# The last tail of a transformer block: projections planned among the value products, transposes two to a bank, fewer idle products, a fourth bank for the up products

## The chip, the cores and the metric

The kernel runs on one core of one Trainium2 chip. The metric is the device time of one launch in microseconds, median of three runs. Beside it one execution was recorded by the hardware profiler; all times within the kernel are taken from that one, counted from the start of its span.

## The reference

One transformer block on 2048 tokens of width 512, in bf16. A vector c gives six modulation rows; the first half is attention with 32 heads of 16, the second a dense layer pair with a GELU between:

```
mod = silu(c) @ w_mod            -> sa, ca, ga, sb, cb, gb
h = layernorm(x) * (1 + ca) + sa
x = x + ga * (softmax(q k^T / 4) v) @ wo      with q, k, v from h @ wqkv
h = layernorm(x) * (1 + cb) + sb
out = x + gb * (gelu(h @ w1 + b1) @ w2 + b2)  with 1376 inner columns
```

## The kernel before

**The stream.** The tokens are four blocks of 512. For each block the 32 heads are treated in eight groups of four, so there are 32 groups ("quads", `nq` = 32). A group needs scores against 16 tiles of keys. Twelve of these tiles go through ScalarE's exponential in units of three and two banks (tiles sA and sB in PSUM, pA and pB out of them, lines 1063 and 1115); the others through an approximation on VectorE (lines 1181 and 1210, tile t), whose scores go into one of two single banks called aux. The value products (`do_pv`, line 1267) add everything up in one bank called od. When a group is done, its od is divided by its denominators and becomes a tile OT.

**The planner.** Python code plays through the whole attention with assumed durations and writes the instructions in the order in which it would start them. At each step `pe_step` chooses what TensorE gets: scores, value products, a step of a "job", or, if nothing is due, `do_fill` (line 1290): four products of zeros into od, which only keep TensorE busy. Jobs are everything else: projections of q, k and v, and for each finished block its tail (output projection, layer norm, both dense layers). A job has a due time `at`, counted in groups, a list of steps, and labels that it needs; a job that holds an aux bank keeps any other such job from starting. The chip then runs each engine's queue in the written order, with waits on semaphores between engines.

**The last block.** Its tail can't hide behind later attention. Two jobs `last_oproj(0)` and `last_oproj(1)` (due at 31.0 and 31.05) make the output projections of token tiles 0 and 1 in the two aux banks: an identity product that brings in the residual xr, then one product for each OT tile t = 0 to 6 (`o_mm`, lines 741 and 742). The product of t = 7 waits for the last group. `do_out` treats this group apart: the denominators are spread by a shuffle (line 1315), inverted (`recip`, 1318) and multiplied in (`norm`, 1321), first for tokens 0 to 255; the rest is handed to `last_tail` in pieces: `last["recip"]`, `last["norm"]`, and `last["out"]`, which copies od to o_sbL (line 1299) and sends the denominators over two transfers on SP's queue (d, then dall) for a test of their range at the end.

`last_tail` writes the rest by hand. Its order for TensorE before: t = 0 to 6 of token tile 2 in a bank of `fpo`; `keep_on(KEEP[0])`, four idle products into a bank that nobody reads (line 795); t = 7 of tiles 0 and 1; tile 3; six more idle products (`KEEP[1]`). Then the block is treated in two halves of 256 tokens. `norm_half` takes the statistics on VectorE (line 799), copies x1 (the tile xr) on ScalarE (800), and normalizes to hnL (274). `begin_down` (lines 842 and 843) puts the residual and the bias into the output banks. `transposes` turns hnL by chunks of 128 columns (line 279, two products to a chunk) and evacuates them with scale and shift to h2T (316 on ScalarE, 319 on VectorE). `up_half` makes eleven products of 256 tokens (line 817, four instructions each) and a GELU on ScalarE for each (819, tile uG). `down_tile` (line 824, eleven instructions) ends a token tile; it is copied (828 or 830) and stored through SP (831).

The banks of transposes and up products come in turn from the list `own`: three of the pool `fps` (name fb) and od's as the fourth, which is in the turn only once `span[0]` is 4:

```
own = [(fps, "fb"), (fps, "fb"), (fps, "fb"), (psO, "od")]
turn, span = [], [3]
```

The first idle product's bank and each transposed chunk take a place in the turn. The order of the second part is this:

```
norm_half(0); begin_down(0), begin_down(1)
last["recip"](256, 384); transposes(0)
last["recip"](384, 512); last["norm"](256, 512)
up_half(0, range(5)); t = 7 of tiles 2 and 3; norm_half(1)
up_half(0, range(5, 11)); begin_down(2), begin_down(3)
down_tile(0); transposes(1); down_tile(1)
last["out"](); span[0] = 4
up_half(1, range(11)); range_flag(); down_tile(2); flag; down_tile(3)
```

Of the kernel before, what the change touches and what calls it, by code (L numbers as in the profile page):

```python
# [25 lines left out]
NC = 4  # L26
# [33 lines left out]

WARM = 18

KEEP = (4, 6)

POOL_WAIT = 3.0

# [32 lines left out]
def adaln_block(ctx: ExitStack, tc: tile.TileContext, A_x, A_wqkv, A_wo, B_x, B_w1, B_b1, B_w2, B_b2,  # L99
# [644 lines left out]

    def last_oproj(tt):

        def f(part):
            def g(j):
                if part == 0:
                    j.ps = last[tt] = j.alloc()  # L750
                for t in range(2 * part, min(7, 2 * part + 2)):
                    o_mm(j.ps, tt, t)
            return g
        job(8 * NQB - 1.0 + 0.05 * tt, [(PE_, n * MM, f(i)) for i, n in enumerate((3, 2, 2, 1))],
            ["last", "d_done"] + [("ot", NQB - 1, t) for t in range(7)], ("last", tt), 99)

    for tt in range(2):
        last_oproj(tt)
# [2 lines left out]
    def last_tail():  # L761

        b = NQB - 1
        tl, tl2 = late["tl"], late["tl2"]
        W_1, W_2, b1c = late["W_1"], late["W_2"], late["b1c"]
        x1 = last["xr"]
        h2 = tl.tile([P, NC, 512], BF16, name="h2T")
        uG = tl.tile([P, NFC, 512], BF16, name="uG")
        hnp = ctx.enter_context(tc.tile_pool(name="hnp", bufs=2))
        hn2 = [hnp.tile([P, 4, D], BF16, name="hnL") for _ in range(2)]  # L770
        st = tl.tile([P, 4, 6], FP32, name="st2")
        with tc.tile_pool(name="fpo", bufs=2, space=PSUM) as fpo, \
                tc.tile_pool(name="fps", bufs=3, space=PSUM) as fps:

            own = [(fps, "fb"), (fps, "fb"), (fps, "fb"), (psO, "od")]
            turn, span = [], [3]

            def bank(dt=FP32, n=512):
                if not turn:
                    turn.extend(range(span[0]))  # L780
                pool, nm = own[turn.pop(0)]
                return pool.tile([P, n], dt, name=nm)

            early = tl.tile([P, 1], FP32, name="early")
            nc.scalar.activation(out=early, in_=eps_c, func=ACT.Sqrt)
            po = [last[0], last[1]] + [fpo.tile([P, 512], FP32, name="fo") for _ in range(2)]
            for t in range(7):
                o_mm(po[2], 2, t)


            idle = bank()

            def keep_on(n):
                for _ in range(n):
                    nc.tensor.matmul(out=idle, lhsT=ident, rhs=hT[:, 0, 0:512], start=True, stop=True)
            def norm_half(hf):
                tts = (2 * hf, 2 * hf + 1)
                for tt in tts:
                    nc.vector.bn_stats(out=st[:, tt, :], in_=po[tt])
                    nc.scalar.copy(out=x1[:, tt, :], in_=po[tt])  # L800
                mv, rs = (ln_rstd if hf else ln_sqrt)(st[:, 2 * hf:2 * hf + 2, :], 2)
                for i in range(2):
                    ln_norm(x1, hn2[hf], mv, rs, 2 * hf + i, i)

            def transposes(hf):
                for j in range(NC):
                    pst = bank(BF16, 256)
                    transpose_chunk(pst, hn2[hf], j, (2 * hf, 2 * hf + 1))
                    hT_evac(h2[:, j, 256 * hf:256 * hf + 256], pst, 8 + j,
                            "act" if j % 2 and not hf else "dve")  # L810

            def up_half(hf, fcs):
                cs = slice(256 * hf, 256 * hf + 256)
                for fc in fcs:
                    ps = bank(FP32, 256)
                    for j in range(NC):
                        nc.tensor.matmul(out=ps, lhsT=W_1[:, j, fc * P:(fc + 1) * P], rhs=h2[:, j, cs],
                                         start=(j == 0), stop=(j == NC - 1))
                    nc.scalar.activation(out=uG[:, fc, cs], in_=ps, func=ACT.Gelu_apprx_tanh,
                                         bias=b1c[:, fc:fc + 1], scale=1.0)  # L820

            def down_tile(tt, eng=None):
                for fc in range(NFC):
                    nc.tensor.matmul(out=po[tt], lhsT=uG[:, fc, tt * P:(tt + 1) * P], rhs=W_2[:, fc, :],
                                     start=False, stop=(fc == NFC - 1))
                o = tl2.tile([P, D], BF16, name="ob")
                if eng == "act":
                    nc.scalar.copy(out=o, in_=po[tt])
                else:
                    nc.vector.tensor_copy(out=o, in_=po[tt])  # L830
                nc.sync.dma_start(out=out_tok[4 * b + tt], in_=o)

            keep_on(KEEP[0])
            for tt in (0, 1):
                o_mm(po[tt], tt, 7)
            for t in range(7):
                o_mm(po[3], 3, t)
            keep_on(KEEP[1])

            def begin_down(tt):  # L840

                nc.tensor.matmul(out=po[tt], lhsT=ident, rhs=x1[:, tt, :], start=True, stop=False)
                nc.tensor.matmul(out=po[tt], lhsT=ones_row, rhs=late["b2r"], start=False, stop=False)
            norm_half(0)

            nc.scalar.activation(out=early, in_=b1c[:, 0:1], func=ACT.Gelu_apprx_tanh)
            for tt in (0, 1):
                begin_down(tt)
            last["recip"](256, 384)
            transposes(0)  # L850
            last["recip"](384, 512)
            last["norm"](256, 512)
            up_half(0, range(5))
            for tt in (2, 3):
                o_mm(po[tt], tt, 7)
            norm_half(1)
            up_half(0, range(5, NFC))
            for tt in (2, 3):
                begin_down(tt)
            down_tile(0)  # L860
            transposes(1)
            down_tile(1)
            last["out"]()
            span[0] = 4
            up_half(1, range(NFC))
            bad, onec, fl = range_flag()
            down_tile(2)
            pf = bank(FP32, 1)
            nc.tensor.matmul(out=pf[0:1, :], lhsT=bad, rhs=onec, start=True, stop=True)
            nc.vector.tensor_copy(out=fl, in_=pf[0:1, :])  # L870
            down_tile(3, "act")
# [254 lines left out]
    def progress():  # L1126

        return act_prog[0]
# [287 lines left out]
    def pe_step():  # L1416
        m = mode[0]
        ready = qk_ready()
        its = next_unit()
        if its is None or not all(quad_labels(qi, kt) for qi, kt, _ in its):  # L1420
            slack = INF
        else:

            slack = max(act_pending() - 0.45, exp_end.get(unit["u"] - 2, act_pending()) + SEM) - clock
        if ready and (m == "row" or slack < 0.35):
            rows = do_qk()
            if d_ready():
                r = d_row(rows)
                if r is not None:
                    do_d(r, True)  # L1430
            return True
        dr = d_ready()
        if dr and m == "row" and (free[DVE_] <= clock + 0.5):
            do_d(d_row(()), False)
            return True
        todo = pv_list()
        n = len(todo)
        if ready and not (m == "col" and n and slack > 0.5):
            rows = do_qk()
            if dr:  # L1440
                r = d_row(rows)
                if r is not None:
                    do_d(r, True)
            return True
        o = job_for(PE_)
        late_ = o is not None and o.at + 0.3 < progress()
        if o is not None and (late_ or n < 3) and (o.rows[o.i][1] + SWITCH <= slack + 0.25 or late_):
            do_job(o, PE_)
            return True
        if n and (m == "col" or n >= 3 or todo[0][0] + 1.5 < clock):  # L1450
            do_pv(todo[0][1], todo[0][2])
            return True
        if dr and free[DVE_] <= clock + 0.4:
            do_d(d_row(()), False)
            return True
        if o is not None and o.rows[o.i][1] + SWITCH <= slack + 0.3:
            do_job(o, PE_)
            return True
        if n:
            do_pv(todo[0][1], todo[0][2])  # L1460
            return True

        while pe_log and pe_log[0][0] < clock - FILL_SPAN:
            pe_log.popleft()
        return slack > FILL_SLACK and sum(d for _, d in pe_log) < FILL_SHARE * FILL_SPAN and do_fill()
# [106 lines left out]
```

## Time and profile before

| | |
|---|---|
| median of 3 runs | 811.74 us (811.29 to 812.61) |
| the profiled execution | 814.66 us |
| its span | 812.8 us |
| mean granted TensorE clock | 0.991 |
| TensorE products (PE), weight loads (PEld) | 769.4 us busy (95%), 235.2 us (29%) |
| VectorE (DVE), ScalarE (ACT) | 714.6 us (88%), 755.1 us (93%) |
| GpSimd (POOL) | 84.4 us (10%) |

Busy times by stretch of the last part, in microseconds:

| stretch | PE | DVE | ACT | clock |
|---|---|---|---|---|
| 760.0 to 770.0, attention | 9.98 | 9.85 | 10.00 | 1.00 |
| 770.0 to 775.3, first projections | 5.25 | 0.39 | 3.56 | 1.00 |
| 775.3 to 784.0, last group, first half's norm | 8.35 | 6.66 | 3.14 | 1.00 |
| 784.0 to 792.0, up products of the first half | 6.85 | 5.33 | 6.64 | 1.00 |
| 792.0 to 803.0, down, up of the second half | 10.18 | 3.26 | 4.05 | 1.00 |
| 803.0 to 812.8, last down tiles, store | 5.18 | 2.71 | 1.38 | 0.91 |

A share over the span says little about this kernel's last part: the stretches have different limits. In a line of the timeline stand start, length, engine, line, operation, tile written and tiles read; "x12" joins instructions that follow one another; brackets give the engine's idle time before it and the engine and line that ended it. Products are pipelined: a product of 512 columns shows 0.38 us, while the next one starts earlier than that.

### The profile page before, as it was taken

How to read it: one execution, taken by the hardware profiler on the slowest of the kernel's cores; microseconds unless marked ns; L12 is line 12 of the kernel's file. 1: busy time of each engine (PE TensorE's matmuls, PEld its weight loads, DVE VectorE, ACT ScalarE, POOL GpSimd, SP SyncE). 2: the span in 40 equal slices, each digit the busy share in tenths (PEclk: the TensorE clock that was granted, in tenths of full speed). 3: DMA queues.
4: the chain of work that ended last, by engine and by line, in shares of the span. 5: the costliest groups of instructions: out<-in, count | busy, mean ns of one | idle time of the engine just before them, and what ended most of it. 6: DMA issues, size and time to landing. Idle time of an engine off the chain costs nothing.

```text
span 812.8 us, 18189 instructions
## 1 busy us (share of the span) xinstructions
PE 769.4 (95%) x7383; PEld 235.2 (29%) x7453; DVE 714.6 (88%) x1260; ACT 755.1 (93%) x681; POOL 84.4 (10%) x126
## 2 busy tenths in 40 slices
PE   6999999997999999999999999999999999999997
PEld 3332222222222223222223222222222322222244
DVE  6779999999998999998999999998997989898752
ACT  4898999997998999999999999999998999999952
POOL 1100002024322000000001000000001000000000
PEclk9999999999999999999999999999999999999999
DMA  9100001022100000000100000000100000000100
GB/s 299 39 1 16 15 16 26 21 94 73 40 16 15 16 15 2 21 23 21 48 15 17 16 14 5 20 22 22 49 15 16 15 13 9 11 28 23 48 0 30
DMA packets 30283, 24.50 MB, mean 30 GB/s; under 512 B 13457, under 2 KB 24050, under 8 KB 30194
## 3 DMA queue, kind: packets, MB, share of 16 engines
q1 hardware_dynamic: 29506, 22.49, 9.6%
q8 instruction: 60, 0.98, 0.5%
q10 hardware_dynamic: 688, 0.79, 0.3%
q14 instruction: 29, 0.24, 0.1%
HBM read 20.65 MB, written 2.61 MB: 29 GB/s over the span
## 4 chain that ended last, share of the span: by engine, by line
PE 53%; ACT 26%; DVE 10%; issue 9%; DMA 2%; POOL 0%; SPq 0%; ACTq 0%; POOLq 0%; DVEq 0%
PE od L1267 16%; ACT pA L1115 13%; ACT pB L1115 10%; PE sA L1063 7%; PE sB L1063 7%; PE aux L1063 4%; DVE t L1210 4%; DVE t L1181 4%; PE aux L713 3%; PE od L1290 3%; PE aux L650 2%; PE aux L688 2%; PE aux L338 1%; ACT uG L702 1%; PE aux L324 1%
## 5 line engine op out<-in xcount | busy, mean ns | idle before, releaser
L1115 ACT ACTIVATE pA<-sA 128x1536 bf16<-128x1536 f32 x309 | 468.3, 1516 | 13.8 <-PE sA L1063 7.0
L1181 DVE TENSOR_SCALAR t<-aux 128x512 int16<-128x512 f32 x504 | 331.8, 682 | 36.6 <-PE aux L1063 35.0
L1115 ACT ACTIVATE pB<-sB 128x1024 bf16<-128x1024 f32 x309 | 336.8, 1090 | 8.2 <-PE sB L1063 4.3
L1210 DVE TENSOR_SCALAR t<-t 128x2048 int16<-128x2048 int16 x378 | 261.1, 713 | 4.0 <-PE od L1267 1.5
L1063 PE MATMUL aux<-qm,kT 32*128 32x512 bf16 x504 | 180.0, 382 | 1.8 <-DVE t L1181 0.8
L1063 PEld LDWEIGHTS <-kT 32*128 32x128 bf16 x2048 | 77.7, 91 | 271.5 <-issue 266.3
L1267 PE MATMUL od<-pB,VE 128*32 128x512 bf16 x617 | 141.4, 388 | 2.8 <-DVE o_sb L1299 2.8
L1267 PE MATMUL od<-pA,VE 128*32 128x512 bf16 x927 | 142.3, 387 | 0.6 <-DVE o_sb L1299 0.5
L1267 PE MATMUL od<-t,VV 128*32 128x512 f16 x1512 | 139.7, 386 | 2.3 <-DVE t L1210 1.9
L1063 PE MATMUL sA<-qm,kT 32*128 32x512 bf16 x927 | 122.6, 384 | 11.9 <-ACT pA L1115 7.7
L1063 PE MATMUL sB<-qm,kT 32*128 32x512 bf16 x617 | 121.4, 385 | 6.3 <-ACT pB L1115 2.6
L1399 POOL COPY mark<-t 1x1 int16<-1x1 int16 x51 | 10.4, 203 | 635.4 <-DVE t L1210 443.5
L1267 PEld LDWEIGHTS <-VE 128*32 128x32 bf16 x2048 | 48.4, 94 | 94.4 <-issue 84.2
L1290 PE MATMUL od<-hT,zeros 128*32 128x512 bf16 x836 | 75.4, 384 | 0.0
L1267 PEld LDWEIGHTS <-VV 128*32 128x32 bf16 x1512 | 40.9, 95 | 57.0 <-issue 46.6
L1267 PE MATMUL od<-t,VE 128*32 128x512 f16 x504 | 50.1, 387 | 1.2 <-DVE o_sb L1299 0.9
L1343 POOL TENSOR_TENSOR OT<-o_sb,rb 128x512 bf16<-128x512 f32 x31 | 39.4, 1271 | 5.4 <-DMA rb<-d 3.9
L713 PE MATMUL aux<-W,uG 128*128 128x512 bf16 x119 | 35.8, 383 | 1.7 <-issue 1.7
L688 PE MATMUL aux<-h2T,W 128*128 128x512 bf16 x113 | 35.4, 384 | 0.7 <-issue 0.6
L1290 PEld LDWEIGHTS <-zeros 128*32 128x32 bf16 x864 | 21.6, 95 | 35.0 <-issue 29.7
L693 DVE TENSOR_SCALAR uG<-aux,b1c 128x512 bf16<-128x512 f32 x33 | 24.6, 744 | 2.3 <-PE aux L688 2.2
L650 PE MATMUL aux<-W_o_pad,OT 128*128 128x512 bf16 x86 | 25.4, 382 | 0.7 <-issue 0.3
(164 smaller groups left out, 433.5 us busy)
## 6 DMA issues: line engine op xcount, KB each, us to landing
rb<-d SPq DMA_DIRECT2D x124, 64.0 KB
W_m<-in_w_mod_dram SPq DMA_DIRECT2D x2, 1024.0 KB
xr<-in_A_x_dram SPq DMA_DIRECT2D x4, 512.0 KB
out_dram<-ob SPq DMA_DIRECT2D x16, 128.0 KB
xb<-in_A_x_dram SPq DMA_DIRECT2D x3, 512.0 KB
W<-in_B_w_dram SPq DMA_DIRECT2D x1, 1376.0 KB
W<-in_B_w_dram SPq DMA_DIRECT2D x1, 1280.0 KB
W_m<-in_w_mod_dram SPq DMA_DIRECT2D x1, 512.0 KB
```

What stands on the lines that cost most here:

```text
L650: nc.tensor.matmul(out=j.ps, lhsT=OT[(b, t)][:, tt * P:(tt + 1) * P], rhs=W_o_pad[:, t, :], start=False, stop=(t == 7))
L688: nc.tensor.matmul(out=j.ps, lhsT=late["W_1"][:, c, fc * P:(fc + 1) * P], rhs=T["h2"][:, c, :], start=(c == 0), stop=(c == NC - 1))
L693: nc.vector.tensor_scalar(out=T["u"][:, fc, :], in0=j.ps, scalar1=late["b1c"][:, fc:fc + 1], scalar2=None, op0=ALU.add)
L713: nc.tensor.matmul(out=j.ps, lhsT=T["u"][:, fc, tt * P:(tt + 1) * P], rhs=late["W_2"][:, fc, :], start=False, stop=(fc == NFC - 1))
L1063: nc.tensor.matmul(out=dst, lhsT=kT[32 * r:32 * r + 32, ch, kt * P:(kt + 1) * P], rhs=qm[(b, ch)][32 * r:32 * r + 32, par, :], start=True, ...
L1115: nc.scalar.activation(out=pt[:, 0:n, :], in_=st[:, 0:n, :], func=ACT.Exp, scale=math.log(2.0) / STEP)
L1181: nc.vector.tensor_scalar(out=t0[(qi, kt)][:, r, :], in0=sd, scalar1=T_BIAS, scalar2=0.0, op0=ALU.add, op1=ALU.max)
L1210: nc.vector.tensor_scalar(out=t16, in0=t0[(qi, kt)], scalar1=float(MJ[j]), scalar2=None, op0=ALU.add)
L1267: nc.tensor.matmul(out=od[qi][32 * r:32 * r + 32, :], lhsT=w, rhs=src, start=first, stop=last_)
L1290: nc.tensor.matmul(out=dst[32 * r:32 * r + 32, :], lhsT=zeros, rhs=hT[:, r, 0:512], start=bank is not None, stop=bank is not None)
L1343: nc.gpsimd.tensor_tensor(out=OT[(b, t)], in0=o, in1=j.rb, op=ALU.mult)
L1399: nc.gpsimd.tensor_copy(out=mark[0:1, 0:1], in_=dve_now["prev"][0:1, 0:1])
```

## The change

- The two `last_oproj` jobs get one step per OT tile instead of two, and stop at t = 5; t = 6 is written in `last_tail`, ahead of the idle products. They need six OT tiles to start instead of seven.
- `pe_step`: when the job at hand is due after `nq - 1.1` (only these two are), value products that are ready go first, and the job is not treated as late.
- `KEEP` falls from (4, 6) to (2, 1).
- `transposes` puts chunks 0 and 2 into one bank and 1 and 3 into another; both chunks of a bank are written ahead of its two evacuations.
- `last["out"]` and `span[0] = 4` move ahead of the first half's up products, and three of these instead of five stand ahead of t = 7 of tiles 2 and 3.

```diff
-KEEP = (4, 6)
+KEEP = (2, 1)
...
-        def f(part):
+        def f(t):
             def g(j):
-                if part == 0:
+                if t == 0:
                     j.ps = last[tt] = j.alloc()
-                for t in range(2 * part, min(7, 2 * part + 2)):
-                    o_mm(j.ps, tt, t)
+                o_mm(j.ps, tt, t)
             return g
-        job(8 * NQB - 1.0 + 0.05 * tt, [(PE_, n * MM, f(i)) for i, n in enumerate((3, 2, 2, 1))],
-            ["last", "d_done"] + [("ot", NQB - 1, t) for t in range(7)], ("last", tt), 99)
+        job(8 * NQB - 1.0 + 0.05 * tt, [(PE_, (1 + (t == 0)) * MM, f(t)) for t in range(6)],
+            ["last", "d_done"] + [("ot", NQB - 1, t) for t in range(6)], ("last", tt), 99)
...
-                for j in range(NC):
-                    pst = bank(BF16, 256)
-                    transpose_chunk(pst, hn2[hf], j, (2 * hf, 2 * hf + 1))
-                    hT_evac(h2[:, j, 256 * hf:256 * hf + 256], pst, 8 + j,
-                            "act" if j % 2 and not hf else "dve")
+                for odd in range(2):
+                    pst = bank(BF16, 512)
+                    for i, j in enumerate((odd, odd + 2)):
+                        transpose_chunk(pst[:, 256 * i:256 * i + 256], hn2[hf], j, (2 * hf, 2 * hf + 1))
+                    for i, j in enumerate((odd, odd + 2)):
+                        hT_evac(h2[:, j, 256 * hf:256 * hf + 256], pst[:, 256 * i:256 * i + 256], 8 + j,
+                                "act" if odd and not hf else "dve")
...
+            for tt in (0, 1):
+                o_mm(po[tt], tt, 6)
             keep_on(KEEP[0])
...
-            up_half(0, range(5))
+            last["out"]()
+            span[0] = 4
+            up_half(0, range(3))
             for tt in (2, 3):
                 o_mm(po[tt], tt, 7)
             norm_half(1)
-            up_half(0, range(5, NFC))
+            up_half(0, range(3, NFC))
             for tt in (2, 3):
                 begin_down(tt)
             down_tile(0)
             transposes(1)
             down_tile(1)
-            last["out"]()
-            span[0] = 4
...
         late_ = o is not None and o.at + 0.3 < progress()
+        if o is not None and o.at > nq - 1.1:
+
+            if n:
+                do_pv(todo[0][1], todo[0][2])
+                return True
+            late_ = False
```

## The prediction

> **What bounds the kernel now.** I read the page first (its clock row and its shares by engine), then the timeline of the last 45 us, because every edit lies there, then the chain of waits for the same stretch, and last the windows of the start, for the clock.
>
> The page's rows say that TensorE is busy 95% of the span and the granted clock stands at 9 tenths or more in every slice. The chain of the last stretch runs almost wholly over TensorE, so here the order of its queue is the time. The timeline shows what stands in that order (start, length, engine, line, tile):
>
> ```profile
> 766.32 0.82 PE L1290 MATMUL od<-hT,zeros 128*32 128x512 bf16 x12
> 768.75 0.60 PE L1290 MATMUL od<-hT,zeros 128*32 128x512 bf16 x8
> 771.32 0.75 ACT L1115 ACTIVATE pB<-sB 128x512 bf16<-128x512 f32 x1
> 775.31 0.40 PE L1267 MATMUL od<-pA,VE 128*32 128x512 bf16 x3
> ...
> 777.38 1.03 PE L795 MATMUL fb<-hT,ident 128*128 128x512 bf16 x4
> 778.06 0.43 DVE L1321 TENSOR_TENSOR OT<-od,rbL 128x256 bf16<-128x256 f32 x1
> 778.54 0.60 PE L742 MATMUL aux<-W_o_pad,OT 128*128 128x512 bf16 x2
> 780.71 1.46 PE L795 MATMUL fb<-hT,ident 128*128 128x512 bf16 x6
> 781.32 0.73 DVE L274 TENSOR_SCALAR hnL<-xr,mv,rs 128x512 bf16<-128x512 bf16 x2
> 783.28 0.51 PE L279 MATMUL fb<-ident,hnL 128*128 128x128 bf16 x6
> ```
>
> The last exponential ends at 771.32 + 0.75 = 772.07, yet the last value products start at 775.31: two whole projection tiles stand ahead of them. OT is ready at 778.49 and its projections (t = 7) start at once. The normalized rows hnL are done at 782.05, but six idle products and the four of begin_down hold TensorE until 783.27.
>
> ```profile
> 784.99 2.02 PE L817 MATMUL fb<-h2T,W 128*128 128x256 bf16 x17 [0.17 <-ACT h2T L316]
> 787.26 1.30 DVE L799 BATCH_NORM_STATS2 st<-fo 128x6 f32<-128x512 f32 x2 [1.61 <-PE fb L817]
> 789.07 2.51 ACT L819 ACTIVATE uG<-fb,b1c 128x256 bf16<-128x256 f32 x6
> 789.61 1.47 PE L817 MATMUL fb<-h2T,W 128*128 128x256 bf16 x12 [0.85 <-ACT uG L819]
> 794.57 0.50 PE L279 MATMUL fb<-ident,hnL 128*128 128x128 bf16 x6
> 795.83 0.27 PE L279 MATMUL fb<-ident,hnL 128*128 128x128 bf16 x2 [0.77 <-DVE h2T L319]
> 798.31 1.91 PE L817 MATMUL fb<-h2T,W 128*128 128x256 bf16 x16
> 805.58 0.08 PEld L869 LDWEIGHTS <-bad 128*1 128x1 bf16 x1 [0.42 <-DVE onec L885]
> 808.26 0.59 ACT L828 CAST ob<-fo 128x512 bf16<-128x512 f32 x1 [4.47 <-PE fo L824]
> ```
>
> The brackets are idle time and its releaser: 0.85 us for a bank held by a GELU, 0.77 us for the bank of the fourth transposed chunk. That the idle products lie on the path, the chain of waits says in a line of its own:
>
> ```profile
> 780.88 1.29 PE fb L795 x6
> ```
>
> For the clock, the windows of the start and of the tail's thinnest stretch (busy time of PE, PEld, DVE, ACT, POOL; then the granted clock, third from the right):
>
> ```profile
> 12.00:13.00 1.00, 0.49 (x2) 0.21 (x2) 1.00 (x3) 1.00 (x2) 0.00 (x0) 0.63 1.10 353
> 13.00:14.00 1.00, 1.00 (x4) 0.34 (x3) 1.00 (x2) 0.35 (x1) 0.00 (x0) 0.50 1.10 350
> 15.00:16.00 1.00, 0.94 (x3) 0.24 (x2) 0.02 (x1) 0.00 (x0) 0.00 (x0) 0.66 1.17 308
> 788.00:790.00 2.00, 1.15 (x11) 0.88 (x10) 1.76 (x9) 1.99 (x5) 0.00 (x0) 1.00 0.00 0
> ```
>
> **Units.** From start to start, a full product of 512 columns takes 0.216 us (eight from 773.49 end at 775.22), one of 256 columns 0.109 us (20 from 798.31 put the next bank's at 800.50), four value products 0.22 us, a change between full, row and column products 0.10 us, and begin_down 1.27 us. I keep a ledger of the lead: how much earlier than before the same event comes.
>
> **1. Projections among the value products.** The built program has 20 filling products fewer; 12 + 8 + 4 become 4 + two gaps used by projections. The first gap: 4 fills (0.22), change (0.10), two products (0.43), change against 12 fills (0.65) and the same last change. The scores sA come some 0.08 us later; ScalarE takes them at 767.76, so this is covered by 0.2 us. The second: one product (0.22), a change, and a value group pulled ahead puts the next sA at about 769.54 instead of 769.37; its exponential at 769.99 needs it by 769.95. The scores are done 0.39 us later, 769.93, a hand-over takes 0.04, so 0.02 us is to spare: 0 to 0.3 us on ScalarE, and I take 0. The bank that the projection takes was read at 765.49 to 766.13, before it is wanted at 766.65. The last value products can then start at 772.22, 3.1 us earlier, and VectorE has OT at 775.41. But TensorE is not free: one product for t = 5, seven for the second tile, eight for po[2], two for t = 6 and two idle ones, 20 x 0.216 = 4.32 us, end at 772.22 + 0.32 + 4.32 = 776.86. So 1.4 us of the 3.1 go into waiting for TensorE, and t = 7 starts at 776.86 against 778.54: **lead 1.68**. POOL's last OT (t = 6) ends at 771.64 and is wanted at 776.
>
> **2. Idle products 6 to 1.** Behind t = 7 come po[3] (8 x 0.216) and one idle product, up to 779.24; the copies that begin_down waits for end at 778.61 and 779.20. Transposes at 779.24 + 1.27 = 780.52; hnL is ready at 782.05 - 1.68 = 780.37. **Lead 2.75** (five idle products are 1.08).
>
> **3. Two transposes per bank.** All eight now run without a wait (0.45 us of starts plus 0.27), but no evacuation starts before the four of its bank are done, where the first began at 783.60, 0.32 after the first transposes. VectorE is not ready anyway: its reciprocal (0.95 us), queued ahead, runs 780.29 to 781.24. ScalarE's two evacuations (0.57 each) start at about 781.15 and end at 782.3; so do the first up products: 782.34 against 784.99. **Lead 2.65.**
> The Trainium skill, "PSUM — Partial Sum Buffer", section "PSUM bank collisions raise a hardware error", says that two engines must not touch one bank at once even at different addresses, which speaks against packing: an evacuation may not overlap the bank's other transposes. By it alone I would add the wait for two more transposes; the row of the reciprocal shows that wait covered on VectorE.
>
> **4. Three up products, then t = 7 of the second half.** Eight 256-column products fewer ahead of it are 0.87 us. VectorE now sets the time: evacuations 781.25 to 781.98, reciprocal to 782.93, OT to 783.30, and then the moved copy o_sbL (0.68) to 783.95, queued ahead of the statistics. Statistics start at 783.95 against 787.26: **lead 3.31**. The copy costs about 0.2 us of that, as the products would let them start at 783.77. Its two transfers pass SP ahead of the output stores; SP has nothing queued from 766.6 to 795.49.
>
> **5. Fourth bank.** The product in od waits for that copy (783.95), behind it three more products, whose GELUs wait on ScalarE behind the two casts, which wait for the statistics: nothing new. The bank that comes free first after the casts is od's, as before fb's: GELU 785.76, TensorE at 786.30 (2.35 us after the statistics, as before). Then four up products remain instead of three: 0.44 us more. **Lead 2.87** at begin_down, 788.04 against 790.91. Here ScalarE's last GELU ends at 789.3, wanted at 791.5.
>
> **6. Second half.** Before, from the transposes (794.57) to the next down tile (795.94) 1.37 us passed; now about 0.50, as each pair has its bank: **lead 3.74**. The four evacuations (1.36) hide behind down_tile(1) (2.37). The flag's 0.1 us at 805.58 may go too, as its transfers, 3.5 us from copy to landing before, now land some 7 us ahead of their reader. Behind that, down tile, cast and store are unchanged.
>
> The sum: 3.75 us off the profiled execution, 814.66 (span 812.8 and 1.86 around it) to 810.9. The median of the runs lies 2.92 under the profiled one; I take the same difference off it: 811.74 - 3.75 = 808.0.
>
> **Rivals.** *VectorE's chain is longer.* Between 777.3 and 785.2 it has hardly a gap in my ledger; each late end moves steps 3 to 5 one for one. If semaphores cost 0.05 us on each of ten steps and the first wait of step 1 costs 0.3 us, 0.8 to 1.5 us go: 809.0 (lead 2.2 to 3.0). For it: every hand-over in the timeline shows 0.02 to 0.05. Against: the same steps before carry them already.
> *The lead dies at the GELUs.* If ScalarE keeps banks longer and the up products of the first half end when they did relative to the exponentials, only steps 1 and 2 less a wait remain: 1.0 to 1.6, so about 810.4, no change that shows.
> *Slower: the clock.* At the start TensorE idles 2.73 us up to 12.51, and about 2.5 us after its last product the granted clock falls to 0.50 for some 3.4 us (windows above): 1.7 us of work lost each time. With fewer idle products a gap of that length in the tail would halve the clock; the lead of 3.75 is gone after 7.5 us at half clock, and it is 0.2% slower after 10.7 us (5.35 us lost). Four such falls in the 22 us after 782 lose 6.8 us: 814.8. It decides from a gap of about 2.5 us; the longest that I find is 1.1 us (781.2 to 782.3, with three products inside), and the 0.85 us gap in 788 to 790 kept 1.00.
> The Trainium skill, "TensorE: Matmul & The Clock Gate", section "Part 1: The HAM clock gate", gives the same gate a free-running window of about 3.4 us, and its section "Part 4: PE-mode transpose" says that transposes do not count as busy. By that, the stretch from the last full product before them (780.5) to the first up product is the dangerous one, 1.8 us; the trace of before has the same stretch (783.3 to 784.99) at clock 1.00.
> *The change doesn't do it*: the built order shows the value products ahead, so only a stall could undo it; that is the second rival.
>
> **Numbers.** Forecast (lead 3.0 to 4.3) 0.63; VectorE's chain 0.20; even more lead 0.05; lead dies 0.07; clock 0.05. A measurement of this kernel can tell 0.2%, 1.6 us. Faster 0.88, same 0.07, slower 0.05. The range reaches from 4.9 us of lead (all waits gone) to 2.0: 806.8 to 809.7.
>
> **What would show it.** Right: last value products at 772.2 to 772.5, t = 7 at about 776.9 with no wait on OT, transposes at 780.5, statistics at 784, no wait of 0.77 in the second transposes, clock 1.00 to the end. Wrong: exponentials ending after 772.4, a wait of the up products beyond 0.5 us at od, or a granted clock under 1.00 before 804.

## The result, and the profile after

The median fell from 812.61 to 806.67 us (11 runs of each; ratio 0.9938, 95% interval 0.9919 to 0.9957). That median lies 0.1 us under the range's lower end, and 5.94 us is more than the 3.75 forecast. A second set, run with the experiments below, gave 810.33 and 806.34 us (ratio 0.9956, 0.9938 to 0.9974): 3.99 us. The profiled execution after took 809.6 us, its span 807.8, so 5.0 us less than before.

Not all of these 5.0 us come from the change. The last instruction that both kernels start alike is a row of six joined shifts on VectorE, at 766.69 us before. After, and in a second profile of the changed kernel (`again`), it stands elsewhere:

```profile
765.73 3.70 DVE L1214 TENSOR_SCALAR t<-t 128x2048 int16<-128x2048 int16 x6
```

```profile
759.35 3.69 DVE L1214 TENSOR_SCALAR t<-t 128x2048 int16<-128x2048 int16 x6
```

On TensorE the two programs are the same up to 0.05 us ahead of this row, where the first projection takes the place of idle fills; on VectorE, ScalarE and GpSimd up to the row itself. So I count from these shifts to the start of the last cast on ScalarE, and call that the tail. It is 41.57 us in the one profile before and 37.52 in both profiles after: the change is worth **4.05 us**. (What follows the cast, mainly a store, takes 4.1 to 4.6 us in the twelve profiles.) The tail's ledger, in us from the shifts:

| event | before | after | lead | lead forecast |
|---|---|---|---|---|
| last value product | 8.63 | 5.59 | 3.04 | 3.09 |
| t = 7, tiles 0 and 1 | 11.85 | 10.23 | 1.62 | 1.68 |
| transposes, first half | 16.59 | 13.88 | 2.71 | 2.75 |
| statistics, second half | 20.57 | 17.00 | 3.57 | 3.31 |
| begin_down, second half | 24.22 | 21.09 | 3.13 | 2.87 |
| up products, second half | 31.62 | 27.56 | 4.06 | 3.74 |
| last cast | 41.57 | 37.52 | 4.05 | 3.75 |

The timeline after, the rows that answer to those shown of before:

```profile
770.45 0.67 ACT L1119 ACTIVATE pB<-sB 128x512 bf16<-128x512 f32 x1
770.78 0.59 PE L742 MATMUL aux<-W_o_pad,OT 128*128 128x512 bf16 x2 [0.16 <-POOL OT L1347]
771.30 0.40 PE L1271 MATMUL od<-pA,VE 128*32 128x512 bf16 x3
774.06 0.42 DVE L1325 TENSOR_TENSOR OT<-od,rbL 128x256 bf16<-128x256 f32 x1
775.53 0.59 PE L794 MATMUL fb<-hT,ident 128*128 128x512 bf16 x2
775.96 0.59 PE L742 MATMUL aux<-W_o_pad,OT 128*128 128x512 bf16 x2
778.72 0.74 DVE L274 TENSOR_SCALAR hnL<-xr,mv,rs 128x512 bf16<-128x512 bf16 x2
779.61 0.62 PE L279 MATMUL fb<-ident,hnL 128*128 128x128 bf16 x8
780.24 0.63 DVE L319 TENSOR_SCALAR h2T<-fb,modc 128x256 bf16<-128x256 bf16 x2
780.60 1.88 PE L819 MATMUL fb<-h2T,W 128*128 128x256 bf16 x12 [0.38 <-DVE h2T L319]
780.78 0.95 DVE L1322 RECIPROCAL rbL<-rbL 128x128 f32<-128x128 f32 x1
782.11 0.68 DVE L1303 COPY o_sbL<-od 128x512 f32<-128x512 f32 x1
782.73 1.29 DVE L798 BATCH_NORM_STATS2 st<-fo 128x6 f32<-128x512 f32 x2
785.08 0.60 PE L819 MATMUL od<-h2T,W 128*128 128x256 bf16 x4 [0.33 <-ACT uG L821]
790.48 0.39 PE L279 MATMUL od<-ident,hnL 128*128 128x128 bf16 x4
790.70 0.39 PE L279 MATMUL fb<-ident,hnL 128*128 128x128 bf16 x4
793.29 1.04 PE L819 MATMUL fb<-h2T,W 128*128 128x256 bf16 x8
803.25 0.59 ACT L830 CAST ob<-fo 128x512 bf16<-128x512 f32 x1 [4.47 <-PE fo L826]
```

The last exponential ends at 771.12 and the last value products follow at 771.30. OT is ready at 774.48, but its projections start only at 775.96, behind planned work and two idle products. The second half's transposes carry no wait. The bracket of 0.16 us on POOL is not a wait: three projections stand there in the program (weights at 770.55), 0.10 + 3 x 0.216 us bring the queue from 770.44 to 771.19, just ahead of the value products, and one record of the three is missing. (In `fill_gaps` below, where all three are recorded, they start 4.82 us from the shifts, as these weights do.) Before, the two evacuations on VectorE took longer:

```profile
783.60 0.73 DVE L319 TENSOR_SCALAR h2T<-fb,modc 128x256 bf16<-128x256 bf16 x2 [0.69 <-PE fb L279]
```

Windows of the tail (the granted clock is third from the right):

```profile
780.00:785.00 5.00, 4.23 (x34) 3.00 (x32) 4.83 (x14) 3.90 (x10) 0.00 (x0) 1.00 0.01 3
785.00:790.00 5.00, 4.92 (x29) 2.73 (x29) 1.59 (x8) 2.59 (x8) 0.00 (x0) 1.00 0.02 2
```

The stretch where VectorE and the evacuations hold TensorE up keeps clock 1.00.

### The profile page after: what moved, and what is told of

The parts are those of the page before. It is cut to its first block, busy times and chain, and to the rows that moved or that the text cites. A ratio compares the mean times of both kernels' runs of the same rounds, so it can differ in the third digit from the quotient of the medians.

```text
span 807.8 us, 18135 instructions
## 1 busy us (share of the span) xinstructions
PE 766.2 (95%) x7355; PEld 234.1 (29%) x7426; DVE 714.1 (88%) x1260; ACT 754.8 (93%) x681; POOL 85.4 (11%) x126
## 4 chain that ended last, share of the span: by engine, by line
PE 51%; ACT 27%; DVE 10%; issue 9%; DMA 2%; POOL 1%; SPq 0%; POOLq 0%; ACTq 0%; DVEq 0%
PE od L1271 16%; ACT pA L1119 14%; ACT pB L1119 10%; PE sA L1067 7%; PE sB L1067 6%; PE aux L1067 4%; DVE t L1214 4%; DVE t L1185 3%; PE aux L713 3%; PE od L1294 2%; PE aux L650 2%; PE aux L688 2%; PE aux L338 1%; ACT uG L702 1%; PE aux L324 1%
```

## The experiments

Each kernel is the changed one with one edit, so that what it loses is what the edit was worth there. "Tail" is as above, 37.52 us for the changed kernel; the first four expectations were written for the span's end, counted from the same shifts (42.07 for the changed kernel), which is given in brackets. Apart from `again` and the last one, each of these kernels ran once.

**The changed kernel again**

> The changed kernel once more, profiled and timed. Measure: the tail, from the start of the six joined shifts t<-t on VectorE (the last instruction that both kernels start alike) to the end of the span: 46.11 us before, 42.07 us in the first profile after. Theory (the ledger of leads is the whole effect): the tail repeats within 0.1 us, so the change is worth 4.0 us in every execution, and what the medians differ beyond it is spread of the part ahead of the tail. Rival (the change also acts ahead of the tail, or the tail itself varies from run to run): a tail that differs by over 0.3 us, or a median difference that stays near 6 us in the new rounds.

The tail repeated to 0.01 us at every event of the ledger. The span's end differs by 0.22 us, all of it behind the cast. Over both sets the medians' difference went from 5.94 to 3.99 us, while the tail did not move. So the tail is the measure of the change, and the 4.05 us lie inside both intervals. The rest of the first 5.94 us is not explained. Of the 3.99 us, the profiled spans make up 3.55 (medians 808.4 and 804.85); the time of a launch around its span fell as well, from a median of 2.1 to 1.5 us, and no profile shows why.

**The planner's edits undone**

> Undone: the planner's edits alone (old last_oproj jobs, old pe_step, t = 6 in the jobs); idle products, transposes and banks stay changed. Ledger: the last value products start 3 us later, OT comes late, t = 7 waits for it again and comes 1.62 us later, and everything behind follows: tail 43.7 us (42.07 + 1.62), with a wait on OT of about 1 us. Rival (the filling products stood only in waits, so projecting in their place moves nothing that counts): tail 42.5 us or less.

```diff
-        job(8 * NQB - 1.0 + 0.05 * tt, [(PE_, (1 + (t == 0)) * MM, f(t)) for t in range(6)],
+        job(8 * NQB - 1.0 + 0.05 * tt, [(PE_, n * MM, f(i)) for i, n in enumerate((3, 2, 2, 1))],
...
-        if o is not None and o.at > nq - 1.1:
...
-            for tt in (0, 1):
-                o_mm(po[tt], tt, 6)
             keep_on(KEEP[0])
```

Tail 39.15 us (43.57): 1.63 us lost, as the ledger says. Its timeline:

```profile
773.66 0.40 PE L1270 MATMUL od<-pA,VE 128*32 128x512 bf16 x3
...
775.73 0.59 PE L795 MATMUL fb<-hT,ident 128*128 128x512 bf16 x2
776.41 0.42 DVE L1324 TENSOR_TENSOR OT<-od,rbL 128x256 bf16<-128x256 f32 x1
776.89 0.60 PE L742 MATMUL aux<-W_o_pad,OT 128*128 128x512 bf16 x2 [0.57 <-DVE OT L1324]
```

The last value product stands behind the projections again (8.64 us from the shifts), OT comes at 11.8, and t = 7 waits for it. The 0.57 us of wait are half of the 1 us expected; the time lost is right all the same, since it is set by OT.

**Six idle products instead of one**

> Undone: the second group of idle products alone (1 becomes 6 again). Ledger: transposes 5 x 0.216 = 1.08 us later, of which 0.1 to 0.2 are covered by VectorE's reciprocal ahead of the evacuations: tail 42.95 to 43.15 us. Rival (VectorE's chain decides behind the transposes, and the idle products stand in its shadow): tail under 42.6 us.

`KEEP = (2, 1)` becomes `(2, 6)`. Tail 38.59 us (42.83): 1.07 lost, the whole of 5 x 0.216. The transposes start 1.07 us later (14.95), and nothing behind them takes any of it up, not even the 0.1 to 0.2 us that were expected of the reciprocal.

**One transposed chunk to a bank**

> Undone: the packing of two transposed chunks in a bank alone. Ledger: the second half's transposes wait again for an evacuation, 0.8 to 0.9 us: tail 42.9 us, all of it in the second half; the first half as in the changed kernel within 0.1 us, as the reciprocal covers it. Rival (with four banks in the turn the fourth chunk finds a free bank in the second half too): no wait there and tail 42.1 us or, as the first evacuation may start earlier in the first half, 41.9 us.

```diff
-                for odd in range(2):
-                    pst = bank(BF16, 512)
...
+                for j in range(NC):
+                    pst = bank(BF16, 256)
+                    transpose_chunk(pst, hn2[hf], j, (2 * hf, 2 * hf + 1))
```

Tail 37.76 us (42.26): 0.24 lost, not 0.8. The rival holds for the second half: its transposes show no wait, and the stretch from them to the up products is 2.82 us against 2.81. The loss is in the first half, where the turn still has three banks, so that the fourth chunk must wait until one of them has been evacuated:

```profile
778.76 0.27 PE L279 MATMUL fb<-ident,hnL 128*128 128x128 bf16 x2 [0.54 <-ACT h2T L316]
```

The fourth chunk is late, ScalarE evacuates it late, the up products start 0.17 us later (their fourth instruction, the first to need ScalarE's second evacuation, 0.24) and the statistics 0.25 us.

**The fourth bank late**

> Undone: last["out"] and the fourth bank, which come only after down_tile(1) again; packing, three up products and all else stay changed. Measure from here on: from the six joined shifts to the start of the last cast on ScalarE, 41.57 us before, 37.52 in both profiles after. Ledger: with three banks the first product that waits for a GELU behind the casts is the seventh, so one more is left after it, 0.44 us, and the flag's transfers come late, 0.1: 38.0 us, with no wait in the second half's transposes, as two packed pairs need only two banks. Rival (the fourth bank, not the packing, took the wait in the second half away): 38.8 us with a wait of 0.8 there.

```diff
-            last["out"]()
-            span[0] = 4
             up_half(0, range(3))
...
             down_tile(1)
+            last["out"]()
+            span[0] = 4
             up_half(1, range(NFC))
```

Tail 37.95 us: 0.43 lost, by the wait for the first GELU behind the casts. The seventh up product has it, and from it on five products remain instead of four:

```profile
781.34 2.34 PE L819 MATMUL fb<-h2T,W 128*128 128x256 bf16 x20 [0.85 <-ACT uG L821]
```

No wait in the second half, and the flag's transfers cost nothing. The statistics start at 17.00 us here too, although the copy o_sbL is not ahead of them, and VectorE waits for TensorE there: the copy cost them nothing.

```profile
779.00 1.29 DVE L798 BATCH_NORM_STATS2 st<-fo 128x6 f32<-128x512 f32 x2 [0.55 <-PE fb L819]
```

**Both undone**

> Undone: packing and fourth bank together. Undoing the packing alone cost 0.24 us and left no wait in the second half. If either of the two is enough to take the wait of 0.77 away (each alone leaves a bank free), it must come back only here: 39.0 us (38.0 + 0.24 + 0.8). Rival (what took the wait away is something else, such as VectorE being free earlier): 38.2 us and no wait.

The two diffs above together. Tail 39.13 us: 1.61 lost, where the two alone lose 0.24 + 0.43 = 0.67. The other 0.94 is the wait of before, back at the same length. (Its bracket, 0.77, counts from the end of the product ahead. Products overlap, and without the wait this one would have started 0.93 us earlier.)

```profile
794.32 0.27 PE L279 MATMUL fb<-ident,hnL 128*128 128x128 bf16 x2 [0.77 <-DVE h2T L319]
```

So either edit is enough to take this wait away; the second of them got nothing for it.

**Five up products ahead of t = 7**

> Undone: five up products instead of three ahead of t = 7 of the second half; the fourth bank stays early. The ledger of step 4 taken alone gives 0.6 us more (0.87 less what VectorE's copy hid): 38.1 us. Rival (with four banks early the two moved products only change sides of the casts: statistics come 0.9 us later, two products fewer remain behind them): 37.6 us.

`range(3)` becomes `range(5)` in both places. Tail 38.03 us: 0.51 lost; the ledger's 0.6 is nearer than the rival's 0.1. The statistics start 1.39 us later, more than two products (0.87), since the product in od waits for the copy (bracket 0.36; its start comes 0.52 us later than right behind the product ahead); two products fewer behind the casts give most of it back.

```profile
780.40 0.60 PE L819 MATMUL od<-h2T,W 128*128 128x256 bf16 x4 [0.36 <-DVE o_sbL L1303]
781.69 1.29 DVE L798 BATCH_NORM_STATS2 st<-fo 128x6 f32<-128x512 f32 x2 [1.34 <-PE fb L819]
```

**A gap on purpose, for the clock**

> The changed kernel with about 4.2 us of extra work on VectorE (seven reciprocals of 64 columns on a scratch tile, then a copy of one column of hnL onto itself) between the first half's normalization and its transposes, so that TensorE stands idle for some 4 us there: the slower rival of the prediction, made on purpose. If the gate works in the tail as at the start (half clock some 2.5 us into a gap, for some 3.4 us), the granted clock reads 0.50 in windows behind the gap, and the last cast starts at 42.7 to 43.4 us, 1.0 to 1.7 more than the delay itself. If a gap of that length leaves the clock alone here: 41.7 us and clock 1.00.

```diff
+            gap = tl.tile([P, 64], FP32, name="gap")
+            nc.vector.memset(gap, 1.0)
+            nc.vector.tensor_copy(out=gap[:, 0:2], in_=hn2[0][:, 1, 0:2])
+            for _ in range(7):
+                nc.vector.reciprocal(out=gap, in_=gap)
+            nc.vector.tensor_copy(out=hn2[0][:, 0, 0:1], in_=hn2[0][:, 0, 0:1])
             last["recip"](256, 384)
             transposes(0)
```

Its timeline and windows:

```profile
780.34 1.01 PE L279 MATMUL fb<-ident,hnL 128*128 128x128 bf16 x8 [4.33 <-DVE hnL L858]
```

```profile
776.00:778.00 2.00, 0.01 (x1) 0.00 (x0) 1.86 (x5) 0.33 (x2) 0.00 (x0) 1.00 0.02 4
778.00:780.00 2.00, 0.00 (x0) 0.00 (x0) 1.90 (x4) 0.00 (x0) 0.00 (x0) 0.53 0.00 0
782.00:784.00 2.00, 2.00 (x10) 1.33 (x10) 1.57 (x3) 1.16 (x3) 0.00 (x0) 0.50 0.00 0
784.00:786.00 2.00, 1.78 (x13) 1.33 (x13) 1.00 (x2) 0.94 (x3) 0.00 (x0) 0.77 0.01 4
```

The transposes start 4.40 us later, the last cast 5.93: 1.53 us more than the delay, at half clock from about 778.1 (0.53 in a window of 2 us leaves 1.88 us of it) to about 784.9. The gate does work in the tail; the clock falls 2.1 us after the last product's end. The Trainium skill, "TensorE: Matmul & The Clock Gate", section "Part 1: The HAM clock gate", names a free-running window of about 3.4 us and puts the half clock "after ≥1 idle window (~3.4µs)". Two such windows fit the 6.8 us at half clock; the fall 2.1 us after the last product is earlier than a whole idle window would have it, and the measurement decides.

**No idle products**

> The changed kernel with KEEP = (0, 0): its three idle products gone, nothing else. Ledger: t = 7 comes 2 x 0.216 = 0.43 us earlier, as OT has 1.46 us to spare; behind that the copies that begin_down needs and hnL move with the statistics, so the third idle product is worth nothing more: last cast at 37.1 us, clock 1.00 as no gap of TensorE reaches 2 us. Rival (the idle products guard the clock): a granted clock under 1.00 in the tail and last cast at 38 us or later.

`KEEP = (0, 0)`. Tail 37.05 us, 0.47 better, and clock 1.00 in the tail: in this run none of the three was needed to hold the clock.

**A step further**

> A step further: no idle products at all; t = 6 of tiles 0 and 1 and half of token tile 2's products stand ahead of t = 7, the rest behind it, so that t = 7 comes when OT is ready; begin_down of the first half stands behind the transposes, where TensorE waited for the evacuations. Ledger: OT is ready at 8.77 us after the shifts, t = 7 of the changed kernel starts at 10.23: lead 1.46; hnL then is done at 12.3 and the transposes start there instead of 13.88; VectorE's reciprocal and evacuations move with the statistics (1.45), begin_down (1.27) fills the gap before the up products. Last cast at 36.1 us against 37.52, and the median some 0.2% under the changed kernel's. Rival (TensorE, with begin_down ahead of the up products, becomes the bound): last cast at 36.6 to 36.9. Rival (without idle products the clock falls): a granted clock under 1.00 in the tail and last cast over 37.5.

```diff
-KEEP = (2, 1)
+KEEP = (0, 0)
...
-            for t in range(7):
+            for tt in (0, 1):
+                o_mm(po[tt], tt, 6)
+            for t in range(3):
                 o_mm(po[2], 2, t)
...
             for tt in (0, 1):
                 o_mm(po[tt], tt, 7)
+            for t in range(3, 7):
+                o_mm(po[2], 2, t)
...
-            for tt in (0, 1):
-                begin_down(tt)
             last["recip"](256, 384)
             transposes(0)
+            for tt in (0, 1):
+                begin_down(tt)
```

Tail 36.41 us, 1.11 better than the changed kernel and 5.16 better than before; median 804.92 against 810.40 us (ratio to before 0.9935, 0.9911 to 0.9959). By the tail it beats both; its median is 0.2% under the changed kernel's 806.34 of the other set, which is within the spread. The last cast came between the expectation (36.1) and the first rival (36.6):

```profile
771.17 0.59 PE L742 MATMUL aux<-W_o_pad,OT 128*128 128x512 bf16 x2
774.49 0.80 PE L279 MATMUL fb<-ident,hnL 128*128 128x128 bf16 x8
776.08 0.39 PE L849 MATMUL aux<-b2r,ones_row 1*128 1x512 bf16 x1
776.39 1.48 PE L821 MATMUL fb<-h2T,W 128*128 128x256 bf16 x12
```

OT was ready at 770.97 and t = 7 started 0.2 us later, behind a product that was already in the queue. begin_down holds the up products until 776.39, when all four evacuations are done. Their first instructions therefore run without the gaps they had, but the fourth, the first to need ScalarE's second evacuation, comes only at 776.73, 14.50 us from the shifts against 15.61: a lead of 1.11, which stays to the end. By an estimate from these rows it could have started some 0.3 us earlier without begin_down ahead of it (776.39), so a part of the first rival holds.

## Why the prediction was right or wrong

- **Step 1** (lead 1.68): measured 1.62, and 1.63 when undone. The main reading held: 3 us of earlier value products, of which half go into a queue that is never free. ScalarE's exponentials came 0.07 to 0.09 us later, inside the 0 to 0.3 given; the last one ended at 5.39 us from the shifts, 5.38 before.
- **Step 2** (five products, 1.08): measured 1.09 in the ledger and 1.07 when undone.
- **Step 3**: the lead at the up products was right (2.69 measured at the first product's fourth instruction, 18.30 against 15.61; 2.65 forecast). But the step read packing in the first half as a later evacuation that the reciprocal covers; undone it loses 0.24 us there, so packing is a gain: with single chunks a bank in use stops the fourth chunk.
- **Step 4** (3.31): 3.57. The term that was mis-sized is VectorE's chain from the first evacuation to the statistics: 2.70 us in the sum, 2.49 measured, and it began 0.05 us earlier. Nearly all of the 0.21 lies in the two evacuations: they took 0.63 instead of 0.73 us, and the reciprocal started 0.09 us before they ended, while the sum laid the rows end to end. So VectorE no longer came last. The step had TensorE's own bound at 783.77 and put it second; the statistics started at 782.73, in that count 783.69, and `bank_late`, with no copy at that place and a wait for TensorE, has the same 17.00. The cost of the copy, 0.2 us, was not there. The 0.26 us stay in the ledger to the end.
- **Step 5** (0.44 given back): 0.44, and the wait for the first GELU behind the casts was where it was put.
- **Step 6** (0.87): 0.93 from begin_down to the up products. The size was right, the cause only half of it: I put it down to packing. `chunk_banks` and `chunk_late` show that packing or the early fourth bank alone takes the wait of 0.77 us away. The step failed by looking at one edit with the other left as it was before. The flag's 0.1 us, which it thought might go too, was not there to win: the lead is 4.06 ahead of the flag and 4.05 behind it.
- **The sum**: 3.75 forecast, 4.05 in the tail; the 0.30 are 0.26 from step 4 and small change. The losses of the edits undone (1.63, 1.07, 1.61 for the two of the banks, 0.51) add up to 4.82, not to 4.05, since each was undone with the others in place. The medians' 5.94 of the first set holds another 1.9 us that no event of the tail shows. The forecast also took the time around the span as unchanged, which it was not: 0.44 of the second set's 3.99 us lie there, so that this figure comes close to 3.75 in part by luck.
- **Rivals**: VectorE's longer chain was the wrong way round, it was shorter. The lead did not die at the GELUs. The clock stayed at 1.00, but `cold_gap` shows that the mechanism is real in the tail. Its price was less than I had: 6.8 us at half clock cost 1.53 us, not 3.4, as the gap itself took up 2.2 of them and TensorE waited for other engines in part of the rest. 2.1 us without a product were enough there, where the prediction had 2.5.

## What to carry to other kernels

Keep a ledger of when the same event comes, not of work removed: here 3 us won at one event were 1.6 at the next, because a queue had other work to do, and idle fillers that once filled a wait became the wait. Where two edits free the same resource, undo them alone and together; undone alone each looked cheap (0.24 and 0.43 us), both together were worth 1.61. And when executions differ by more than the change, measure from the last common instruction: that repeated to 0.01 us where the spans differed by 6.6.

## What the runs showed of the hardware

The spans of one and the same program differ by up to 6.6 us (807.8 and 801.2), and the difference lies almost wholly ahead of the tail. One place is seen in the traces. In the first profile after, TensorE waits 2.13 us for a copy on VectorE, which stands behind a long row of shifts, and around this wait the clock is at half:

```profile
196.07 3.07 DVE L1214 TENSOR_SCALAR t<-t 128x2048 int16<-128x2048 int16 x1
197.19 0.47 PE L1067 MATMUL sA<-qm,kT 32*128 32x512 bf16 x3 [0.35 <-ACT pA L1119]
199.79 0.61 PE L1271 MATMUL od<-pB,VE 128*32 128x512 bf16 x2 [2.13 <-DVE o_sb L1303]
```

```profile
195.00:200.00 5.00, 2.40 (x22) 0.66 (x22) 5.00 (x5) 4.40 (x4) 4.31 (x7) 0.74 0.01 3
197.00:197.50 0.50, 0.31 (x3) 0.09 (x2) 0.50 (x1) 0.50 (x2) 0.50 (x3) 0.88 0.00 0
200.00:205.00 5.00, 4.64 (x28) 0.74 (x22) 4.12 (x7) 1.65 (x2) 0.60 (x2) 0.50 0.02 3
```

In `again`, at the same instructions, the shift and the wait are shorter and the clock stays:

```profile
193.83 1.69 DVE L1214 TENSOR_SCALAR t<-t 128x2048 int16<-128x2048 int16 x1
196.17 0.39 PE L1271 MATMUL od<-pB,VE 128*32 128x512 bf16 x2 [0.82 <-DVE o_sb L1303]
```

```profile
195.00:200.00 5.00, 4.03 (x35) 1.05 (x35) 4.89 (x8) 4.32 (x4) 2.91 (x4) 1.00 0.04 7
```

The wait did not bring the clock down here. It begins at 197.66 (199.79 less 2.13), while the clock fell at about 197.4: 0.88 in the half microsecond from 197.0 leaves 0.12 us at half clock, and the row of three products at 197.19 lasts 0.47 us, where such a row lasts 0.39 at full clock. What made it fall is open. In eleven of the twelve profiles it falls between 194 and 200 us, also in six whose wait at this place is only 0.60 to 0.83 us; in `again`, with 0.82, it does not.

How long the wait is follows the shift on VectorE. It mostly takes 0.68 us, but 3.06 to 3.07 in `before`, `after` and `chunk_late`, where two products of GpSimd (1.15 us each) run meanwhile, and 1.68 to 1.69 in `again`, `keep_six` and `fill_gaps`, where one does. No run moved these products, so that they are the reason is not shown.

How `after` falls behind `again` can be followed: 2.2 us at the wait before this one (192.60 against 190.36), 3.6 here, 6.9 when the clock is full again (208.21 against 201.33), 6.4 at the shifts. Half of it thus comes in the 10.2 us at half clock, from 197.4 to 207.6. In the other profiles too the shifts start later, on the whole, the more time at half clock lies ahead of them: from 759.35 with none (`again`) and 761.1 and 762.0 with 6.8 us to 767.63 with 20.5 (`chunk_late`). That the two go together is all that these traces show; the share of the waits is not separated from it.
